# Block 1's second layer by seven half products, the turned keys of pairs 13 to 15 copied by ScalarE

## The chip, the core and the metric

The kernel runs on one core of one Trainium2 chip. The core's engines work side by side and wait for each other through semaphores: TensorE (PE in the profile, with its weight loads shown apart as PEld), VectorE (DVE), ScalarE (ACT), GpSimd (POOL) and SyncE (SP). Each engine takes its instructions strictly in the order in which the program lists them. SP and POOL also issue the DMA transfers; a DMA issue that has to wait holds up everything behind it in its engine's queue. The metric is the time in microseconds (us) of one execution of the whole program on the device, the median of several runs.

## What is computed

Eight batches (B) of eight heads (H) with 576 tokens (S) and 64 values a head. Attention over 16 "beacon" keys and the causal part of the 576 keys, then a mixer over the tokens of low rank (32), then a two-layer network of 512, 2048 and 512 channels:

```python
scores = scale * np.matmul(q, k_all.transpose(0, 1, 3, 2))   # k_all: 16 beacon keys, then 576
scores = np.where(causal, -1000000000.0, scores)
a = np.exp(scores - scores.max(-1, keepdims=True)); a /= a.sum(-1, keepdims=True) + 1e-09
x = np.matmul(a, v_all)                 # heads side by side: (8, 576, 512)
h = x.transpose(0, 2, 1) @ U @ V        # over the tokens, rank 32
u = x + h.transpose(0, 2, 1)
out = u + np.maximum(u @ w_ch1, 0.0) @ w_ch2
```

## The kernel before, in words

**Two kinds of work, interleaved by hand.** Attention goes by pairs of heads: four pairs (c = 0 to 3) in each of eight batches make pairs 0 to 31. The network goes by blocks of 512 tokens: nine blocks, 0 to 8, counted through all batches, so that block 1 needs batches 0 and 1. The work of a block is cut into units that stand in a list (`queue`); `fill(n)` takes the next n of them and emits their instructions. The attention's steps are written out by hand, and between them stand the fills: in `play` a letter f is one unit, q and k turn a pair's queries and keys, v is scores and exponentials, a and b are the two heads' products with the values, m is masks, r is a regrouping. A program order on every engine follows from that. `mix(b)` puts the mixer's units of batch b into the list and appends the blocks that become computable (`feed`).

**Turning queries and keys.** For pairs up to 15 a pair's queries and keys are first copied close together by VectorE (`regroup`, L290 and L292), then turned by TensorE into PSUM (L297), then copied from PSUM to `qT` and `kT` (`qkT_units`, L330; the 16 beacon columns by L335). `copies` in `qkT_of` says which engine copies: `copies[0]` is for the keys, `copies[1]` for the queries. Later batches are turned by DMA (`turns`, L869, on SP).

**A plain block** (`mlp_units`; blocks 0 and 1 before the change, by `FAST = 2` at L957). First layer: 16 units of four matmuls of 512 columns (L751), each with a Relu to f16 by ACT (L764) or DVE (L766). Second layer: 16 units of four matmuls of 512 columns (L777), 64 matmuls; four sums with the residual by DVE (L790; in block 0, copies by L792 and L794) and four stores by SP (L796), one for each 128 tokens.

**A fast block** (`fast_units`; blocks 2 to 8). The first layer is the same (L607, L618, L616). The second layer is a product of 2 x 2 quarters by seven half products instead of eight: A, F, B, C, D, E and D again, each of two units of eight matmuls of 256 columns (L633), 112 matmuls. They need sums of quarters of the hidden layer on DVE (L596, placed by the table `SUMS`), sums of quarters of the weights (`halves_of_w2`, L560, eight DVE instructions, once for the program, hung on units 16, 18, ... 30 of the last plain block) and sums of the products (`after`): one copy by ACT (L666), six sums by DVE (L654), then for each of four output tiles a sum with the residual by POOL (`residual`, L654 on POOL) and two stores by SP (`store`, L658). The units of the second layer are 14, of a plain block 16.

**What stands in SP's and POOL's queues around block 1.** POOL issues the loads of later batches: values (L239), beacons (L221), keys and queries (L852). These come one with each fill (`coming`). SP issues the stores, the DMA turning of the residual (`ut`, L583 or L745), the turning of keys and queries (L869), and the turning of attention's output `xb` into `uT` (L455, five instructions a batch), to which DVE adds the mixer's result (L476).

The lines that set this:

```python
            if t < FAST:
                units, state["part"] = mlp_units(512 * t, 512, dst, t % 2, t > 0)
                if t == FAST - 1:
                    for i, u in zip(range(NDC, 2 * NDC, 2), halves_of_w2()):
                        units[i] = lambda a=units[i], u=u: (a(), u())
            else:
                units = fast_units(512 * t, dst, t == NBLK - 1)
```

Of the kernel before, what the change touches and what calls it, by code (L numbers as in the profile page):

```python
# [30 lines left out]
def kernel(  # L31
# [21 lines left out]
    NH2 = H // 2  # L53
# [241 lines left out]
    def in_pair(pr):  # L295

        return [lambda ps, o, n, j, t=t: nc.tensor.transpose(ps[:, ds(o, n)], t[:n, j, :, :], ident[:n, :n]) for t in pr]  # L297

    def by_heads(st, c):

        def turn(ps, o, n, j, t):
            for h in range(2):
                nc.tensor.transpose(
                    ps[ds(D * h, D), ds(o, n)], t[:n, 2 * c + h, ds(D * j, D)], ident[:n, :n]
                )

        return [lambda ps, o, n, j, t=t: turn(ps, o, n, j, t) for t in st]
# [11 lines left out]
    def qkT_units(turns, qT, kT, c, copies=((nc.vector.tensor_copy,), (nc.vector.tensor_copy,)), apart=None):  # L319

        def one(i, dst, b0):
            w = TJ // len(copies[i])
            bs = 0 if apart else b0
            whole = dst[:, c, b0 : b0 + S].rearrange("x (p j) -> x p j", j=TJ)
            for a, copy in enumerate(copies[i]):
                ps = pst([P, TP * w + bs], F16, name="tps")
                for j in range(w * a, w * a + w):
                    n = TP + bs if j == TJ - 1 else TP
                    turns[i](ps, TP * (j - w * a), n, j)
                copy(  # L330
                    out=whole[:, :, ds(w * a, w)],
                    in_=ps[:, 0 : TP * w].rearrange("x (j p) -> x p j", j=w),
                )
                if bs and a == len(copies[i]) - 1:
                    copies[i][0](out=dst[:, c, 0:b0], in_=ps[:, TP * w : TP * w + b0])  # L335
                emptying(ps)
            if b0 and apart:
                beacons_apart(apart, dst, c, copies[i][0])

        return [lambda: one(1, qT, 0), lambda: one(0, kT, Nb)]  # L340
# [213 lines left out]
    def halves_of_w2():  # L554

        b11, b12 = w2[:, 0:HF, 0:HC], w2[:, 0:HF, HC:DM]
        b21, b22 = w2[:, HF:NDC, 0:HC], w2[:, HF:NDC, HC:DM]
        t1, t2, t3, t4 = (wt[:, i, :, :] for i in range(4))
        return [
            lambda o=o, x=x, y=y, h=h: nc.vector.tensor_tensor(  # L560
                out=o[:, ds(HF // 2 * h, HF // 2)], in0=x[:, ds(HF // 2 * h, HF // 2)],
                in1=y[:, ds(HF // 2 * h, HF // 2)], op=ALU.subtract,
            )
            for h in range(2) for o, x, y in ((t1, b12, b11), (t3, b22, b12), (t2, b22, t1), (t4, b21, t2))
        ]
# [332 lines left out]
    def regroup_of(p):  # L898
        b, c = divmod(p, NH2)
        prs[p] = [regroup(Ls[b][0], c, i, nc.vector.tensor_copy) for i in range(2)]  # L900
# [13 lines left out]
    def new_qT_of(p):  # L914
        b, c = divmod(p, NH2)
        if b not in qTs:
            new_qT(b)

    def qkT_of(p):
        b, c = divmod(p, NH2)  # L920
        new_qT_of(p)
        copies = [(act_copy, nc.vector.tensor_copy) if p == 0 else (nc.vector.tensor_copy,)] * 2
        turns = by_heads(Ls[b][0], c)
        for i, t in enumerate(prs.get(p, ())):
            if t is not None:
                turns[i] = in_pair(prs[p])[i]
        return qkT_units(turns, qTs[b], kTs[b % 2], c, copies, Ls[0][0][0] if p == 0 else None)
# [26 lines left out]
    DT0 = 4  # L954
    LAG = 10
    HINT = 5
    FAST = 2  # L957
    SUMS = {
# [14 lines left out]
    def fill(n):  # L973
        while n > 0 and queue:
            u = queue.pop(0)
            if u is not None:
                u()
            if coming:
                coming.pop(0)()
            n -= 1  # L980

    def feed(b):

        while state["t"] < NBLK and 512 * (state["t"] + 1) <= S * (b + 1):
            t = state["t"]
            dst = lambda i, m, t=t: rows[ds(512 * t + P * i, m), :]
# [27 lines left out]
    def play(line):  # L1014

        for word in line.split():
            what, p = word[0], int(word[1:].split(":")[0] or 0)
            if what == "f":
                fill(1)
            elif what in "qk":  # L1020
                qkT_of(p)["qk".index(what)]()
            elif what == "r":
                regroup_of(p)
            elif what in "ab":
                if what == "a":
                    avs[p] = av_of(p)
                avs[p]["ab".index(what)]()
            elif what in "mno":
                units = scores_of(p)
                units[2]() if what == "m" else units[3]("no".index(what))  # L1030
            elif what == "e":
                scores_of(p)[int(word[-1]) // 2]()
            elif what == "v":
                visit([(int(x[: x.index(":")]), int(g)) for x in word[1:].split(",") for g in x[x.index(":") + 1 :]])

    with tc.manual_schedule(engines={ENG.PE, ENG.Activation, ENG.DVE, ENG.SP, ENG.Pool}):
# [7 lines left out]
        prs[0][0] = regroup(first, 0, 0, V, act_copy, beacons=False)  # L1044
        idle(IDLE[0], plain)
        t0, sc = qkT_of(0), scores_of(0)
        t0[0]()
        idle(IDLE[4], ident)
# [3 lines left out]
        for u in qkT_of(1):  # L1052
            u()
# [83 lines left out]
        fill(8)  # L1137
        regroup_of(NP1)
        regroup_of(NP1 + 1)
        fill(8)  # L1140
        play("q8 f k8 f f v8:01 q9 f k9 f r10 v8:23,9:0 f")
        tr = []

# [206 lines left out]
```

## Time and profile before

| what | us |
|---|---|
| median of 3 runs | 343.74 |
| lowest and highest run | 340.02, 344.1 |
| the profiled execution, as timed | 340.93 |
| its span in the profile | 339.3 |
| busy in that span: PE, DVE, ACT, POOL | 329.8, 234.1, 178.7, 136.1 |

The profile is of one execution. A row of a timeline has start, duration and the instruction, with the idle time ahead of it in brackets and what ended it. A row of the chain of work has start, length and the instruction. A row of the groups by line has count, busy time and the mean of one in ns, then the idle time before. DMA issues stand under the queue that issues them (SPq, POOL); "DMA to landing" is from issue to the data's arrival. The clock of TensorE was granted in full (1.0) throughout. A matmul's duration in a row is longer than its distance to the next one, since matmuls are pipelined; the chain's rows give the distance.

### The profile page before, as it was taken

Reading aid. Unit: us, or ns where it says so; the run is one execution under the profiler, and the core shown is the slowest. Engines: PE = TensorE matmul, PEld = TensorE weight load, DVE = VectorE, ACT = ScalarE, POOL = GpSimd, SP = SyncE. Lnnn points to the kernel's source line nnn. Section 1 sums busy time; section 2 is a strip of 40 time slices with the busy share of each in tenths; the row PEclk is TensorE's granted clock in tenths of the full one; section 3 lists DMA queues with packets and bytes.
Section 4 is the critical chain, followed back from the end, with each engine's and each line's share of the span. In section 5 each row is a group of like instructions: output and inputs, shape, how many; then the busy total and the mean of one; then the engine's idle time right before and its main releaser. Section 6 shows DMA issues by size and latency. Waiting matters only on the chain.

```text
span 339.3 us, 8838 instructions
## 1 busy us (share of the span) xinstructions
PE 329.8 (97%) x3494; PEld 212.0 (62%) x3494; DVE 234.1 (69%) x585; ACT 178.7 (53%) x383; POOL 136.1 (40%) x175
## 2 busy tenths in 40 slices
PE   8799999999999999999999999999999999999993
PEld 4465655455555456865688888755875675585493
DVE  6586885689989748765876677687776963743652
ACT  5957951478851677257734784468445403502500
POOL 8986724765140900677066805040130014013041
PEclk9999999999999999999999999999999999999999
DMA  8999999999997994999999999944213304104113
GB/s 159 141 175 138 183 196 194 200 192 139 138 118 152 153 141 86 101 169 157 151 112 155 187 143 104 132 140 87 66 64 93 73 31 126 31 33 124 31 37 99
DMA packets 150832, 41.97 MB, mean 124 GB/s; under 512 B 132096, under 2 KB 149696, under 8 KB 150784
## 3 DMA queue, kind: packets, MB, share of 16 engines
q0 software_dynamic: 87568, 18.18, 74.6%
q1 hardware_dynamic: 62992, 22.87, 37.4%
q8 instruction: 29, 0.48, 0.6%
q10 hardware_dynamic: 224, 0.30, 0.3%
q14 instruction: 19, 0.16, 0.2%
HBM read 37.45 MB, written 9.44 MB: 138 GB/s over the span
## 4 chain that ended last, share of the span: by engine, by line
PE 88%; DMA 4%; POOL 3%; DVE 1%; issue 1%; ACT 1%; POOLq 0%; DVEq 0%
PE gps L607 29%; PE po L427 9%; PE mpsD L633 7%; PE cps L777 7%; PE gps L751 7%; PE sps L409 5%; DMA vs<-in_v_dram 4%; PE mpsF L633 4%; PE mpsC L633 4%; PE mpsA L633 4%; PE mpsB L633 4%; PE mpsE L633 3%; POOL vs L239 1%; PE sps L370 1%; POOL st L224 1%
## 5 line engine op out<-in xcount | busy, mean ns | idle before, releaser
L418 ACT ACTIVATE expt<-sps 128x496 f16<-128x496 f32 (+2 forms) x192 | 82.0, 539 | 52.6 <-PE sps L409 52.6
L607 PE MATMUL gps<-uT,w 128*128 128x512 f16 (+1 forms) x512 | 103.7, 353 | 0.0
L654 POOL TENSOR_TENSOR ob<-ob,ut 128x512 f32<-128x512 f32 x26 | 30.8, 1188 | 139.9 <-DVE ob L654 127.7
L633 PEld LDWEIGHTS <-gT 128*128 128x128 f16 x800 | 75.1, 98 | 11.3 <-issue 2.1
L618 ACT ACTIVATE gT<-gps 128x512 f16<-128x512 f32 x84 | 49.7, 609 | 58.8 <-PE gps L607 54.3
L607 PEld LDWEIGHTS <-w 128*128 128x128 f16 x512 | 47.6, 98 | 41.4 <-issue 1.6
L239 POOL DMA_DIRECT2D vs<-in_v_dram x50 | 39.7, 804 | 15.3 <-DMA w<-in_moe_w_ch_dram 12.3
L596 DVE TENSOR_TENSOR gT<-gT 128x1024 f16<-128x1024 f16 (+2 forms) x77 | 39.5, 540 | 4.2 <-ACT gT L618 3.3
L427 PEld LDWEIGHTS <-expt 128*128 128x128 f16 x900 | 33.9, 98 | 10.9 <-issue 2.7
L427 PE MATMUL po<-vs,expt 128*128 128x65 f16 x900 | 36.5, 194 | 1.1 <-DMA vs<-in_v_dram 1.0
L616 DVE TENSOR_SCALAR gT<-gps 128x512 f16<-128x512 f32 x28 | 19.3, 691 | 24.0 <-PE gps L607 23.4
L436 DVE TENSOR_TENSOR xb<-po,rec 128x320 f16<-128x320 f32 x64 | 31.4, 491 | 2.2
L751 PE MATMUL gps<-uT,w 128*128 128x512 f16 x128 | 32.5, 379 | 0.1
L777 PE MATMUL cps<-w,gT 128*128 128x512 f16 x128 | 31.1, 379 | 0.0
L435 DVE RECIPROCAL rec<-po 128x5 f32<-128x5 f32 x64 | 12.1, 189 | 19.0 <-PE po L427 18.7
L346 DVE TENSOR_TENSOR expt<-expt,bigmask 128x512 f16<-128x512 f16 x54 | 22.5, 417 | 1.2 <-ACT expt L418 1.2
L409 PE MATMUL sps<-qT,kT 64*128 64x80 f16 (+4 forms) x288 | 22.6, 281 | 0.0
L376 ACT ACTIVATE expt<-sps 128x496 f16<-128x496 f32 (+2 forms) x48 | 20.4, 564 | 0.6 <-PE sps L370 0.6
L409 PEld LDWEIGHTS <-kT 64*128 64x128 f16 x288 | 10.2, 94 | 13.4 <-issue 9.3
L777 PEld LDWEIGHTS <-gT 128*128 128x128 f16 x128 | 11.2, 98 | 11.6 <-issue 1.3
L852 POOL DMA_DIRECT2D st<-in_q_dram x20 | 16.9, 874 | 3.2 <-DVE expt L348 1.4
L751 PEld LDWEIGHTS <-w 128*128 128x128 f16 x128 | 10.6, 97 | 10.8 <-issue 1.2
(125 smaller groups left out, 384.8 us busy)
## 6 DMA issues: line engine op xcount, KB each, us to landing
out_dram<-ob SPq DMA_DIRECT2D x55, 128.0 KB, 1.9
vs<-in_v_dram POOLq DMA_DIRECT2D x18, 128.0 KB, 7.9
w<-in_moe_w_ch_dram POOLq DMA_DIRECT2D x4, 512.0 KB, 6.4
w<-in_moe_w_ch_dram POOLq DMA_DIRECT2D x2, 1024.0 KB, 12.8
out_dram<-ob SPq DMA_DIRECT2D x8, 256.0 KB, 4.9
st<-in_k_dram POOLq DMA_DIRECT2D x12, 128.0 KB, 7.2
st<-in_q_dram POOLq DMA_DIRECT2D x12, 128.0 KB, 8.3
st<-in_k_dram POOLq DMA_DIRECT2D x4, 288.0 KB, 11.9
```

The costliest lines, as they stand in the source:

```text
L239: nc.gpsimd.dma_start(out=dst[a : a + nq[j], j, :, :], in_=src[hs, ds(q0[j], nq[j]), :].rearrange("h p d -> p h d"))
L409: nc.tensor.matmul(banks[i][:, ds(at0 + o, w)], kT[hp, c, ds(P * ch, P)], qT[hp, c, ds(qa, w)], start=True, stop=True, skip_group_check=le ...
L418: nc.scalar.activation(out=at[p][3][i][:, ds(SLOT * g, gw[g])], in_=bank[:, ds(at0, gw[g])], func=AF.Exp, scale=scale)
L427: nc.tensor.matmul(po[:, j, :], ex[0 : nk[c], ds(blk[(c, j)], P)], vs[0 : nk[c], ds(c * H * E + h * E, E)], start=(c == 0), stop=(c == j),)
L436: nc.vector.tensor_tensor(out=xb[:, :, ds(h * D, D)], in0=po[:, :, 0:D], in1=r.broadcast_to([P, NT, D]), op=ALU.mult)
L596: nc.vector.tensor_tensor(out=o[:, ds(d0, n)], in0=x[:, ds(d0, n)], in1=y[:, ds(d0, n)], op=op)
L607: nc.tensor.matmul(g[:, ds(o, w)], w1[:, cc, ts(dc, P)], uT[:, cc, ds(at, w)], start=(cc == 0 and o == 0), stop=(cc == NCC - 1), skip_grou ...
L618: nc.scalar.activation(out=cell["g"][:, dc, :], in_=g, func=AF.Relu)
L633: nc.tensor.matmul(ps, a()[:, d, ds(P * i, P)], bm[:, d, ds(c0, w)], start=fresh and d == 0 and (i == 0 or key != bank), stop=d == HF - 1, ...
L654: eng.tensor_tensor(out=out, in0=x, in1=y, op=ALU.add)
L751: nc.tensor.matmul(g[:, 0:n], w1[:, cc, ts(dc, P)], uT[:, cc, ds(r0, n)], start=(cc == 0), stop=(cc == NCC - 1))
L777: nc.tensor.matmul(ps[:m, :], gT["t"][:, dc, ds(P * i, m)], w2[:, dc, :], start=(dc == 0), stop=turned and dc == NDC - 1, skip_group_check ...
```

## The change

Three edits. `FAST` becomes 1, so that block 1 is a fast block: its second layer is done by the seven half products, and the eight sums of the weights' quarters move to the units of block 0's second layer. The keys of pairs 13, 14 and 15 (`p > (DT0 - 1) * NH2` is p > 12) are copied from PSUM by ACT instead of DVE. The fill after the regroupings of pairs 8 and 9 is 6 units long instead of 8, since a fast block has two units fewer.

```diff
@@ -920,6 +920,8 @@
         b, c = divmod(p, NH2)
         new_qT_of(p)
         copies = [(act_copy, nc.vector.tensor_copy) if p == 0 else (nc.vector.tensor_copy,)] * 2
+        if p > (DT0 - 1) * NH2:
+            copies[0] = (act_copy,)
         turns = by_heads(Ls[b][0], c)
@@ -954,7 +956,7 @@
-    FAST = 2
+    FAST = 1
@@ -1137,7 +1139,7 @@
         fill(8)
         regroup_of(NP1)
         regroup_of(NP1 + 1)
-        fill(8)
+        fill(6)
         play("q8 f k8 f f v8:01 q9 f k9 f r10 v8:23,9:0 f")
```

In the changed program, with block 1 fast, SP's queue has eight half stores (L658) where four whole ones (L796) stood, and POOL's queue has four more sums. POOL's queue then reads: the beacons of the keys of batch 5, the sum of the first output tile, the five key loads and the first query load, the second tile's sum, two query loads, the third tile's sum, the last two query loads, the fourth tile's sum. SP's queue reads: the eight stores, one `ut` turning, then the turning of keys (one) and queries (four), three more of `ut`, and then the five of `xb` (L455) for the next blocks. TensorE has 48 matmuls and 48 weight loads more than before.

## The prediction

> **What bounds the kernel now.** I read the page's shares first, then the waits of TensorE, then the chain of work and the windows around block 1.
>
> ```profile
> span 339.3 us, 8838 instructions
> PE 329.8 (97%) x3494; PEld 212.0 (62%) x3494; DVE 234.1 (69%) x585; ACT 178.7 (53%) x383; POOL 136.1 (40%) x175
> PE 88%; DMA 4%; POOL 3%; DVE 1%; issue 1%; ACT 1%; POOLq 0%; DVEq 0%
> ```
>
> TensorE is busy 97% of the span and holds 88% of the chain that ended last. A saved matmul is saved time only as long as nothing that TensorE waits for comes late. The windows show how much room there is: columns are PE, weight loads, DVE, ACT and POOL busy, then clock, DMA share and GB/s.
>
> ```profile
> 50.25:69.50 19.25, 19.25 (x164) 10.31 (x160) 11.89 (x26) 6.18 (x14) 10.62 (x14) 1.00 1.72 203
> 69.50:94.70 25.20, 24.68 (x315) 13.69 (x312) 22.04 (x64) 20.16 (x46) 12.35 (x16) 1.00 2.09 146
> 94.70:113.40 18.70, 18.70 (x168) 9.43 (x165) 17.75 (x42) 7.44 (x19) 5.83 (x8) 1.00 1.39 135
> 113.40:148.10 34.70, 34.70 (x374) 22.85 (x373) 23.91 (x57) 20.79 (x46) 13.08 (x16) 1.00 1.40 116
> PE tps L297 <- DVE gT L766: 0.5, 1, 0.5
> ```
>
> They are the second layer of block 0, the first and the second layer of block 1, and all of block 2. TensorE has no gap in three of them, and 0.5 us behind DVE in the other. So the stretch of the change gains what TensorE saves, and what comes late there or behind it costs in full.
>
> **The change, part by part.**
>
> *The matmuls.* From the chain of work (start, length):
>
> ```profile
> 107.55 2.59 PE cps L777 x12
> 132.77 1.75 PE mpsA L633 x16
> ```
>
> A matmul of 512 columns takes 2.59 / 12 = 0.216, one of 256 columns 1.75 / 16 = 0.109. Block 1 gives up 64 x 0.216 = 13.8 and gets 112 x 0.109 = 12.25: **-1.57 us**. The first layer keeps its matmuls.
>
> [...]
>
> *The weights' sums on DVE, moved into block 0's second layer.*
>
> ```profile
> L560 DVE TENSOR_TENSOR wt<-w 128x1024 f16<-128x1024 f16 x4 | 2.7, 680 | 0.0
> L596 DVE TENSOR_TENSOR gT<-gT 128x1024 f16<-128x1024 f16 x35 | 23.5, 683 | 3.4 <-ACT gT L618 3.3
> L596 DVE TENSOR_TENSOR gT<-gT 128x768 f16<-128x768 f16 x21 | 11.4, 553 | 0.6
> L596 DVE TENSOR_TENSOR gT<-gT 128x256 f16<-128x256 f16 x21 | 5.5, 287 | 0.2
> L790 DVE TENSOR_TENSOR ob<-cps,ut 128x512 f32<-128x512 f32 x4 | 2.7, 686 | 0.6 <-PE cps L777 0.6
> L330 DVE COPY kT<-tps 128x576 f16<-128x576 f16 x15 | 11.3, 751 | 1.6 <-PE tps L297 0.7 <-PE tps L303 0.7
> ```
>
> Eight at 0.68 = 5.4 us join 11.89 in the window of 19.25: 17.3, still under. What hides them is DVE's idle time there. If an insertion delays a turned key by its length, TensorE waits 0.7; all eight badly placed would be 5.4. I take 0, because the one wait of this kind in the trace is 0.5, and keep 0 to 5.4 for the range. Below zero is excluded, since TensorE has no gap in that window.
>
> *The hidden layer's sums on DVE in block 1.* 35 / 7 = 5, 3 and 3 of the three sizes: 3.4 + 1.7 + 0.9 = 6.0, and six sums of products at 0.69 = 4.1. Away go four L790 (2.7), two Relus (12 L766 in two blocks is six each, a fast block has four: 1.4), the eight weight sums (5.4) and three key copies at 0.75, with their beacon columns (0.16 each: 2.7). Net -2.1 on DVE in the stretch 69.5 to 113.4, where it was busy 39.8 of 43.9. Cost 0: DVE's idle 4.1 hides it. If a sum of the hidden layer is late at its product, TensorE waits for that one piece, 0.29 to 0.68.
>
> *The shorter fill.* Pairs 8 to 15 take their steps up to two units earlier (1.7). The loads that they read do not come earlier, and one regrouping was just in time:
>
> ```profile
> 66.42 9.05 DMA vs<-in_v_dram
> 75.49 0.68 DVE pr L292
> ```
>
> A wait of up to 1.7 on DVE could come of it. TensorE's next reader stood 0.5 behind it already, so the bounds are 0 and 1.7; I take 0, since the chain names a transfer of values there and not the keys' own.
>
> *The key copies on ACT.* The trace has no such copy of 576 columns. The nearest are ACT's Relu of 512 columns at 0.609 and the 96 x 384 copy at 0.523, so 0.5 to 0.75 each, and a second instruction of at most 0.37 (its exponential of 208 columns): at most 3.4 for three. ACT was busy 27.6 of 43.9. Such a copy may stand behind a run of exponentials of 2.9 (six of them at 92.86 in the timeline):
>
> ```profile
> L618 ACT ACTIVATE gT<-gps 128x512 f16<-128x512 f32 x84 | 49.7, 609 | 58.8 <-PE gps L607 54.3 <-issue 4.3
> L893 ACT ACTIVATE pr<-stkq 96x384 f16<-96x384 f32 x2 | 1.0, 523 | 1.0 <-DMA stkq<-in_q_dram 0.7 <-DMA stkq<-in_k_dram 0.3
> L418 ACT ACTIVATE expt<-sps 128x208 f16<-128x208 f32 x48 | 13.2, 368 | 37.1 <-PE sps L409 37.1
> 92.86 2.91 ACT L418 ACTIVATE expt<-sps 128x496 f16<-128x496 f32 x6
> ```
>
> Its reader is the pair's scores, several units of 0.86 later. I take 0; the bounds are 0 and one run of exponentials, 2.9.
>
> *The four sums on POOL and the eight stores on SP.* Here I expect the bill. POOL's sums stand between the loads of batch 5; SP's stores wait for them, and behind the stores stand the turning of keys and queries and then of `xb` (L455), which DVE's L476 needs. First POOL, SP, then DVE and PE of the trace before:
>
> ```profile
> 114.31 4.22 POOL L852 DMA_DIRECT2D st<-in_q_dram  x5
> 138.02 1.15 POOL L654 TENSOR_TENSOR ob<-ob,ut 128x512 f32<-128x512 f32 x1 [13.54 <-DVE ob L654]
> 139.12 4.23 POOL L239 DMA_DIRECT2D vs<-in_v_dram  x5
> 109.62 0.54 POOL L221 DMA_DIRECT2D st<-in_beacon_k_dram  x1 [12.87 <-DMA kT<-st]
> 114.29 0.33 SPq L796 DMA_DIRECT2D out_dram<-ob  x1
> 146.49 5.30 SPq L658 DMA_DIRECT2D out_dram<-ob  x8
> 114.71 1.24 SPq L583 DMA_TRANSPOSE ut<-uT  x1
> 117.35 1.19 SPq L869 DMA_TRANSPOSE kT<-st  x1
> 120.80 5.94 SPq L869 DMA_TRANSPOSE qT<-st  x4
> L455 SPq DMA_TRANSPOSE uT<-xb x5: 1250/1264/1803, 131.2 to 137.0; - x5
> 139.94 2.41 DVE L476 TENSOR_TENSOR uT<-ups,uT 128x496 f16<-128x496 f32 x4
> 142.89 0.68 DVE L654 TENSOR_TENSOR kept<-mpsC,kept 128x512 f32<-128x512 f32 x1
> 144.69 0.69 PE sps L409 x8
> ```
>
> POOL: the beacon load is released by turned keys, which stand behind attention's output on SP; that comes up to two first-layer units earlier (1.7 us), so at 107.9 instead of 109.6. From there 0.54, a sum of 1.15, five key loads and one query load at 0.84 (5.1), a sum, two loads (1.7), a sum, two loads, a sum: 13.5, to 121.4. SP: the last two stores wait for that and take between 0.33 (a store at 114.29) and 0.66 (5.30 for eight), 1.0 for both, to 122.4; `ut` 1.24, keys 1.25: the first query turning issues at 124.9 instead of 120.80, **4.1 late**. L455 follows in the same queue; its fourth, at 137.0 - 1.3 = 135.7, moves to 139.8. L476 waits for the fourth (the fifth is for the short end). TensorE meanwhile is 1.57 early: DVE wants L476 at 139.94 - 1.57 = 138.4.
>
> How long does such a turning take to land? Three stretches show it: beside value loads (issued from 92.6), in quiet, and the key turnings beside value loads (from 139.12).
>
> ```profile
> 92.56 4.19 POOL L239 DMA_DIRECT2D vs<-in_v_dram  x5 [0.38 <-issue]
> DMA to landing us min/median/max: 4.5/5.6/8.2
> DMA to landing us min/median/max: 2.3/2.5/2.9
> DMA to landing us min/median/max: 2.3/7.2/8.3
> ```
>
> The changed program issues value loads at 139.12 - 1.57 = 137.5, so the fourth L455 now falls 2.3 behind their start. Before, it was 3.4 ahead. Quiet ends: 142.3, DVE waits 3.9. Beside loads, 5.6 to 8.3: 145.4 to 148.1, a wait of 7.0 to 9.7. What is queued behind L476 on DVE: the sum of product C, whose bank the scores at 144.69 take. It ended at 142.89 + 0.68 = 143.57, so 1.1 of lateness is covered and the rest stops TensorE: 2.8 in quiet, 5.9 to 8.6 beside loads. I take 6.8 (a landing of 6.5, between the two contended medians 5.6 and 7.2), because the row nearest in time is contended.
>
> [...]
>
> **Sum.** -1.57 + 6.8 = +5.2 against this execution: 340.93 + 5.2 = 346.1. The median shown is 2.8 above this execution, and with three runs I can't say how much of that is chance; I put a third of it on top: **347.0**.
>
> **Rivals.**
> - *The turnings land as in quiet.* For it: value loads may be slow to start. Then -1.57 + 2.8 = +1.2: 342.1. [...] The trace speaks against (7.2).
> - *Faster: the lateness stays within its cover, and the saving stands.* Place: L476; it decides if the fourth L455 lands before 138.4 + 1.1 = 139.5, that is if SP is late by under 1.3 instead of 4.1. For it: block 2 before has the same eight stores behind POOL's sums, and TensorE does not wait in the next stage. Against it: in that stage SP's list has L455 ahead of the keys and queries, here behind. Time 340.93 - 1.57 = 339.4, up to 342.2 on the median.
> - *Worse: another wait on top*, the weights' sums delaying the turned keys of pairs 8 and 9 (up to 5.4), keys on ACT behind exponentials (2.9), or a regrouping that waits for its load (1.7). For it: 17.3 of 19.25 on DVE. Against: DVE idles between these very copies. About 3 to 5 more: 349.5 to 352.
>
> **How the numbers follow.** Chances: forecast 0.5, quiet 0.2, faster 0.17, worse 0.13. The range reaches from inside the faster case to the contended upper bound on the median, 343.74 - 1.57 + 8.6 = 350.8: 341 to 351; it leaves out the lower half of the faster case and most of the worse one. The forecast's own range is 345 to 351. About 2% (6.9 us) can be told from no change: over 2% slower needs the upper end of the forecast or the worse case, 0.17; over 2% faster nothing gives, 0.01; within 0.82.
>
> **What would show it.** Right: 112 matmuls at L633 in block 1 at 0.109; the query turning of SP near 125; a DVE idle of some 7 us ahead of L476 near 138, ended by the DMA of `uT`; TensorE idle by 5 to 8 us between 140 and 150, put down to DVE at L476. The stretch up to block 2 shorter by 1.6. Wrong: L476 without idle ahead, value loads or L455 issued at other times, TensorE's gaps in block 0's second layer or at pairs 13 to 15.

## The result, and the profile after

The changed kernel takes **351.16 us** (median of five runs, 350.98 to 353.0), the kernel before 343.74 (five runs, 340.02 to 348.03). The ratio is **1.0271, 95% interval 1.0203 to 1.0339**: slower by 2.7%, where 347.0 and a range of 341 to 351 were forecast. The kernel before spreads widely, so all ratios here leave the longest executions of a kernel out, while medians keep them.

The profiled execution took 351.16, with a span of 349.5. First the page of the changed kernel: its span, and the rows of TensorE's busy share and granted clock in 40 slices (a slice is 8.7 us).

```profile
span 349.5 us, 8964 instructions
PE   8899999999999999279999999999999999999992
PEclk9999999999999999969999999999999999999997
```

Two slices stand out. The one that starts near 140 has TensorE at 2 tenths, and the next has the clock at 6 tenths. Next, what TensorE and then DVE waited for in the changed kernel (us in total, times, longest).

```profile
PE mpsE L633 <- DVE uT L476: 8.1, 1, 8.1
PE tps L297 <- DVE pr L290: 0.9, 2, 0.7
```

```profile
DVE uT L476 <- DMA uT<-xb: 11.2, 1, 11.2
```

That is the forecast's chain: TensorE waits for L476 on DVE, and that waits for the turned `xb`. Now the queues behind it, POOL and SP in the timeline of the changed kernel (start, duration, and in brackets the idle time ahead), with the landing times of L455.

```profile
109.68 0.54 POOL L221 DMA_DIRECT2D st<-in_beacon_k_dram  x1 [14.53 <-DMA kT<-st]
122.09 1.25 POOL L654 TENSOR_TENSOR ob<-ob,ut 128x512 f32<-128x512 f32 x1
137.70 4.21 POOL L239 DMA_DIRECT2D vs<-in_v_dram  x5
```

```profile
111.47 12.71 SPq L658 DMA_DIRECT2D out_dram<-ob  x8
126.97 5.97 SPq L869 DMA_TRANSPOSE qT<-st  x4
136.96 7.93 SPq L455 DMA_TRANSPOSE uT<-xb  x5
DMA to landing us min/median/max: 6.1/7.2/8.0
```

POOL's last sum ends at 123.34. SP's eight stores hold the queue for 12.71 us, up to 124.18, since the last of them waits for that sum. The query turnings then issue at 126.97 (120.80 before), and L455 starts at 136.96 (131.19 before), beside the value loads of 137.70. It lands in 7.2 instead of 2.5.

Where the 10.2 us between the two spans (349.5 and 339.3) lie is read from five rows of TensorE's timeline: the first products of the first layer in blocks 0, 2 and 3, product E of block 2 and the last product D. Before, then after:

```profile
23.12 1.02 PE L751 MATMUL gps<-uT,w 128*128 128x512 f16 x4
113.36 1.03 PE L607 MATMUL gps<-uT,w 128*128 128x512 f16 x4
143.66 1.04 PE L633 MATMUL mpsE<-wt,gT 128*128 128x256 f16 x8
147.95 1.03 PE L607 MATMUL gps<-uT,w 128*128 128x512 f16 x4
332.16 1.93 PE L633 MATMUL mpsD<-w,gT 128*128 128x256 f16 x24
```

```profile
22.59 1.02 PE L751 MATMUL gps<-uT,w 128*128 128x512 f16 x4
111.90 1.03 PE L607 MATMUL gps<-uT,w 128*128 128x512 f16 x4
150.49 1.87 PE L633 MATMUL mpsE<-wt,gT 128*128 128x256 f16 x8 [8.13 <-DVE uT L476]
156.92 1.03 PE L607 MATMUL gps<-uT,w 128*128 128x512 f16 x4
341.14 1.93 PE L633 MATMUL mpsD<-w,gT 128*128 128x256 f16 x24
```

| stretch | before | after | difference |
|---|---|---|---|
| start to block 0's first layer | 23.12 | 22.59 | -0.53 |
| from there to block 2 | 90.24 | 89.31 | -0.93 |
| block 2 to block 3 | 34.59 | 45.02 | **+10.43** |
| block 3 to the last product | 184.21 | 184.22 | +0.01 |
| from there to the end of the span | 7.14 | 8.36 | +1.22 |

The whole bill lies in one stage, and two small sums beside it were not in the forecast: a gain of 0.93 instead of 1.57, and an end that is 1.22 longer.

### The profile page after: what moved, and what is told of

The parts are those of the page before. It is cut to its first block, busy times and chain, and to the rows that moved or that the text cites. A ratio compares the mean times of both kernels' runs of the same rounds, so it can differ in the third digit from the quotient of the medians.

```text
span 349.5 us, 8964 instructions
## 1 busy us (share of the span) xinstructions
PE 330.5 (95%) x3542; PEld 216.8 (62%) x3542; DVE 238.1 (68%) x590; ACT 182.0 (52%) x392; POOL 140.6 (40%) x179
## 4 chain that ended last, share of the span: by engine, by line
PE 87%; DMA 4%; DVE 3%; POOL 2%; issue 1%; SPq 1%; ACT 1%; DVEq 0%; POOLq 0%
PE gps L607 32%; PE po L427 8%; PE mpsD L633 8%; PE sps L409 6%; PE mpsF L633 4%; PE mpsB L633 4%; PE mpsA L633 4%; PE mpsE L633 4%; PE gps L751 4%; PE cps L777 4%; PE mpsC L633 4%; DMA uT<-xb 2%; DMA vs<-in_v_dram 1%; PE tps L297 1%; PE sps L370 1%
## 5 line engine op out<-in xcount | busy, mean ns | idle before, releaser
L607 PE MATMUL gps<-uT,w 128*128 128x512 f16 (+1 forms) x576 | 120.0, 355 | 0.2 <-DVE xb L436 0.2
L654 POOL TENSOR_TENSOR ob<-ob,ut 128x512 f32<-128x512 f32 x30 | 35.3, 1180 | 151.2 <-DVE ob L654 125.4
L618 ACT ACTIVATE gT<-gps 128x512 f16<-128x512 f32 x96 | 57.1, 611 | 63.8 <-PE gps L607 57.6
L607 PEld LDWEIGHTS <-w 128*128 128x128 f16 x576 | 52.8, 98 | 46.5 <-issue 2.0
L596 DVE TENSOR_TENSOR gT<-gT 128x1024 f16<-128x1024 f16 (+2 forms) x88 | 45.5, 542 | 4.2 <-ACT gT L618 3.3
L616 DVE TENSOR_SCALAR gT<-gps 128x512 f16<-128x512 f32 x32 | 22.1, 691 | 24.4 <-PE gps L607 23.8
L633 PE MATMUL mpsE<-wt,gT 128*128 128x256 f16 x128 | 17.0, 282 | 8.1 <-DVE uT L476 8.1
L476 DVE TENSOR_TENSOR uT<-ups,uT 128x496 f16<-128x496 f32 x24 | 14.5, 666 | 11.7 <-DMA uT<-xb 11.2
L852 POOL DMA_DIRECT2D st<-in_k_dram x20 | 16.9, 856 | 0.7 <-DMA st<-in_q_dram 0.7
L751 PE MATMUL gps<-uT,w 128*128 128x512 f16 x64 | 16.2, 379 | 0.1
```

The lines of the kernel that those rows point to most:

```text
L596: nc.vector.tensor_tensor(out=o[:, ds(d0, n)], in0=x[:, ds(d0, n)], in1=y[:, ds(d0, n)], op=op)
L607: nc.tensor.matmul(g[:, ds(o, w)], w1[:, cc, ts(dc, P)], uT[:, cc, ds(at, w)], start=(cc == 0 and o == 0), stop=(cc == NCC - 1), skip_grou ...
L618: nc.scalar.activation(out=cell["g"][:, dc, :], in_=g, func=AF.Relu)
L633: nc.tensor.matmul(ps, a()[:, d, ds(P * i, P)], bm[:, d, ds(c0, w)], start=fresh and d == 0 and (i == 0 or key != bank), stop=d == HF - 1, ...
L654: eng.tensor_tensor(out=out, in0=x, in1=y, op=ALU.add)
L751: nc.tensor.matmul(g[:, 0:n], w1[:, cc, ts(dc, P)], uT[:, cc, ds(r0, n)], start=(cc == 0), stop=(cc == NCC - 1))
```

## The experiments

The theory: POOL's sums hold SP's stores, these hold the turnings (first keys and queries, then `xb`), and `xb` now lands beside the value loads; L476 comes late, and TensorE stands still. Rivals: the copies on ACT cost it; the sums of the weights do; the loss is work and not waiting; or only one of lateness and contention matters.

### Each link of the chain by itself

*b_noact* takes the copies on ACT out of the changed kernel:

```
-        if p > (DT0 - 1) * NH2:
-            copies[0] = (act_copy,)
```

> The changed kernel with the key copies of pairs 13 to 15 back on DVE. Queue theory (POOL's sums hold SP's stores, these hold the turning of xb at L455, TensorE stands still for L476): the copies play no part, so the wait for mpsE at L633 stays at 8.1 us within 1 and the time stays within 0.5% of the changed kernel's 351.2. Rival (copies on ACT cost it): the wait shrinks and up to 3 us come back, 348.

Measured: 352.17, ratio 1.0316 (1.0256 to 1.0375); the wait for L476 is 7.2. The copies play no part in the loss that can be measured.

*c_turns* changes only the order of SP's queue: the five turnings of batch 5's first keys and queries go behind those of `xb`.

```
-            if c in (0, NH2 - 1) and b + 1 == DT0:
+            if c == 0 and b + 1 == DT0:
                 fill_turns(tr, NT)
```

> The changed kernel with the five turnings of batch 5's first keys and queries (L869) put behind the turnings of xb (L455) in SP's queue, not ahead of them. Queue theory: L455 issues from about 126 to 130 instead of 136.96, ends ahead of the value loads of 137.70, and lands some 2.5 us after issue; L476 no longer waits, TensorE's 8.1 us of idle and the about 2.3 us at half clock behind it go: 351.2 - 10.4 = 340.8, a ratio to before of 0.99 to 1.00. A price can come up where the turned queries are then wanted, since they turn later. Rival (the turnings of xb are late for another reason, or the loss is work and not waiting): the ratio stays at 1.02 or above.

Measured: 341.53, ratio **0.9996** (0.9968 to 1.0023). SP and TensorE in its timeline:

```profile
123.05 6.10 SPq L583 DMA_TRANSPOSE ut<-uT  x4
129.27 6.86 SPq L455 DMA_TRANSPOSE uT<-xb  x5
136.31 1.92 SPq L869 DMA_TRANSPOSE kT<-st  x1
```

```profile
142.04 1.04 PE L633 MATMUL mpsE<-wt,gT 128*128 128x256 f16 x8
146.33 1.03 PE L607 MATMUL gps<-uT,w 128*128 128x512 f16 x4
```

L455 has been issued before the value loads begin (137.54) and lands in 2.5 (median), and product E runs without idle ahead of it. From 111.75, its first product of block 2, the stage takes 34.58, as before. One place in a queue is worth ten microseconds, and no price of the later queries shows: from block 3 to the last product it is 184.36 (184.21 before).

*d_vlate* leaves SP late but issues batch 5's value loads one slot later, so that L455 lands alone.

```
-            if c == (1 if b >= DT0 else 0) and b + 1 < B:
+            if c == (2 if b == DT0 else 1 if b >= DT0 else 0) and b + 1 < B:
                 load_batch(b + 1)
```

> The changed kernel with batch 5's value loads issued one slot later, so that the turnings of xb no longer land beside them; SP's lateness stays. If lateness and contention share the bill: the landing of L455 falls from 7.2 to about 2.5, L476 starts some 4.8 us earlier, TensorE's idle falls from 8.1 to about 3.3, and if the half clock behind it comes of a long idle, its 2.3 go as well: 344 to 346. If lateness alone does it: the idle stays at 8 and the time at 351. If contention alone does it: no idle, 341. The later values can cost something of their own where block 3 begins.

Measured: 347.98, ratio 1.0206 (1.0131 to 1.0281). The landing falls to 2.5, DVE's wait from 11.2 to 5.4, TensorE's idle to 2.33: lateness and contention share the bill, as expected. But the clock was expected to stay up with the shorter idle, and it did not, so the time misses the 344 to 346. First the landing times of L455, then rows of TensorE's timeline, then its windows (length, busy time, matmuls, granted clock, DMA share, GB/s):

```profile
DMA to landing us min/median/max: 2.4/2.5/3.2
```

```profile
144.68 1.54 PE L633 MATMUL mpsE<-wt,gT 128*128 128x256 f16 x8 [2.33 <-DVE uT L476]
152.77 1.03 PE L607 MATMUL gps<-uT,w 128*128 128x512 f16 x4
```

```profile
142.00:144.00 2.00, 0.35 (x4) 1.00 0.53 106
144.00:146.00 2.00, 1.32 (x8) 0.76 0.25 45
146.00:148.00 2.00, 2.00 (x8) 0.50 0.65 128
150.00:152.00 2.00, 2.00 (x11) 0.53 0.59 167
152.00:154.00 2.00, 2.00 (x26) 1.00 0.68 210
```

TensorE is busy again from 144.68, and the clock still halves: at 146 - 2 x (1 - 0.76) / 0.5 = 145.04, until 150 + 2 x 0.47 / 0.5 = 151.88, which is 6.84 us. So here the half clock falls on work, and takes back 1.96 (table below) of what the shorter idle saved.

*e_dve* makes block 1's four residual sums on DVE, so that the stores do not wait for POOL.

```
-            add(obs[name], obs[name], u_of(h, c), nc.gpsimd)
+            add(obs[name], obs[name], u_of(h, c), nc.vector if t0 == 512 else nc.gpsimd)
```

> The changed kernel with block 1's four residual sums on DVE instead of POOL (4 of about 0.7, 2.8 us of DVE work more). Queue theory: SP's last stores no longer stand behind POOL's loads, SP's L455 comes back to about 132 to 135, ahead of the value loads, and the wait of 8.1 at mpsE goes nearly or wholly, the half clock with it: 341 to 344. Rival (SP is held by the stores' number or the turnings' order, not by POOL's sums): L455 still issues at 137, and the time stays at 350 or above.

Measured: 342.86 (runs of 340.88 to 350.79), ratio 1.0026 (0.9982 to 1.007); no wait for L476 in the profiled execution. Its SP:

```profile
119.32 6.43 SPq L869 DMA_TRANSPOSE qT<-st  x4
130.84 6.42 SPq L455 DMA_TRANSPOSE uT<-xb  x5
```

With the same eight stores in the same place, L455 is at 130.84 (before: 131.19). It is POOL's sums between its loads that hold SP, not the number of stores.

### How much the clock costs

*h_fill* (on the changed kernel, 64) and *i_fill* (on d_vlate, 18) put matmuls of zeros into TensorE's idle; they add zero to product D's bank.

```
+            if k == 4 and j == 1 and t0 == 1024:
+                for _ in range(64):
+                    nc.tensor.matmul(
+                        banks["D"][0 : NC * P - SK, 0, :], kTs[0][:, 0, SK : NC * P], w2[:, 0, 0:HC],
+                        start=False, stop=True, skip_group_check=True,
+                    )
```

> The changed kernel with 64 matmuls of zeros (48 columns wide, 256 rows moved, added to product D's bank) behind product D's first half of block 2, where TensorE stands idle for 8.1 us. At 0.109 each they fill 7.0 of it. Nothing waits less: L476 is as late as before. Clock theory (TensorE's idle halves its own clock for 6.8 us, worth about 2.3 here): the granted clock stays 1.00 from 140 to 160, and 2 us come back: 349. Rival (the clock falls for another reason, or zeros do not count): the clock is 0.50 from 147 to 154 as before, and the time stays at 351 or above. If the matmuls lengthen the path themselves, 353 or more.

Measured: 348.48, ratio 1.0204 (1.0123 to 1.0286), and the clock row has no dip. The number is as expected, but the trace says that little of it is the clock; that the number fits is luck. The clock row of its page, then TensorE and DVE in its timeline:

```profile
PEclk9999999999999999999999999999999999999998
```

```profile
111.49 1.03 PE L607 MATMUL gps<-uT,w 128*128 128x512 f16 x4
141.87 7.17 PE L721 MATMUL mpsD<-w,kT 128*48 128x256 f16 x64
148.09 2.42 DVE L476 TENSOR_TENSOR uT<-ups,uT 128x496 f16<-128x496 f32 x4 [9.95 <-DMA uT<-xb]
148.97 1.05 PE L633 MATMUL mpsE<-wt,gT 128*128 128x256 f16 x8
150.56 0.37 PE L409 MATMUL sps<-qT,kT 64*128 64x496 f16 x1 [0.24 <-DVE uT L476]
151.78 0.75 PE L409 MATMUL sps<-qT,kT 64*128 64x464 f16 x2 [0.21 <-DVE kept L654]
155.10 1.03 PE L607 MATMUL gps<-uT,w 128*128 128x512 f16 x4
```

From product E to block 3's first product, the kernel before takes 147.95 - 143.66 = 4.29. h_fill takes 155.10 - 148.97 = 6.13 **at full clock**, the changed kernel 156.92 - 150.49 = 6.43 at half. So 1.84 of the 2.1 lost there is DVE's backlog: the scores trickle behind L476 and the sum of product C, one bank at a time. In the changed kernel the half clock costs 0.3 at most. Of the 3.0 between the two spans (349.5 and 346.5), 1.41 lie in this stage, where L476 was late by 9.95 and not 11.20; 1.18 are a shorter end, and 0.41 lie ahead of block 2.

> The kernel with batch 5's value loads one slot later (347.98; TensorE idle 2.3 us for L476, then 0.50 of the clock for 6.83 us from 145.05), with 18 matmuls of zeros put into that idle (18 x 0.109 = 2.0). Clock theory: the half clock is what the rest of its loss is made of, 6.83 x 0.5 = 3.4 us: with the idle filled the clock stays 1.00 and the time falls by 3.4 to about 344.5. Rival (an idle this short does not halve the clock, something else does): clock and time stay as they are, 348.

Measured: 346.75, ratio 1.0127 (1.0034 to 1.022), runs of 345.16 to 349.33. The profiled execution (347.91) has 0.7 of idle left, and its clock halves nonetheless, later, from 148.2 to 155.0. The runs at a mean clock of 0.997 and 0.993 took 345.16 and 345.58, near the 344.5 expected; those at 0.990 and 0.989 took 347.91 and 349.33. So the size of the clock's part fits. What brings the half clock on is not shown: here the longest idle ahead of it was 0.72, while h_fill kept its clock with gaps of 0.2 to 0.3, and the rival (something else than the idle halves it) is not refuted.

### Single parts on the kernel before

*f_halves* only moves the weights' sums into block 0 (`if t == FAST - 1` becomes `if t == 0` with FAST still 2); *a_act* only has the two lines of b_noact added.

> The kernel before with one part of the change: the eight sums of quarters of the second layer's weights (L560) are made between block 0's second-layer units and not block 1's; block 1's second layer stays whole products. Theory (the price forecast as 0 was a wait of some 0.7 at a regrouping of turned keys in block 0): a ratio of 1.000 to 1.003, and a wait of TensorE for DVE's pr of 0.5 to 1 us between 60 and 70. Rival (it costs up to its work, 5.4): a ratio of up to 1.016.

> The kernel before with one part of the change: the key copies of pairs 13 to 15 on ACT. Forecast and theory: no effect, a ratio within 0.997 to 1.003. Rival (copies behind exponentials, up to 2.9 us): a ratio of up to 1.008, with a wait of TensorE's scores for ACT's kT.

Measured: f_halves 345.71, ratio 1.002 (0.9973 to 1.0066); a_act 342.94, ratio 0.9981 (0.9926 to 1.0036). Neither part moves the time by what can be measured, and the wait for `pr` between 60 and 70 that was expected in f_halves is not there. Their profiled executions (348.16 and 347.57) are longer than their medians and show something else. f_halves, DVE and TensorE:

```profile
144.75 2.42 DVE L476 TENSOR_TENSOR uT<-ups,uT 128x496 f16<-128x496 f32 x4 [5.65 <-DMA uT<-xb]
```

```profile
112.44 1.03 PE L607 MATMUL gps<-uT,w 128*128 128x512 f16 x4
145.47 1.03 PE L633 MATMUL mpsE<-wt,gT 128*128 128x256 f16 x8 [2.58 <-DVE uT L476]
154.40 1.30 PE L607 MATMUL gps<-uT,w 128*128 128x512 f16 x4
```

This program has no stores behind POOL's sums, and yet the same wait. Its POOL got to L221 at 111.05, and SP's query turnings issued at 124.10 instead of 120.80: 3.3 us were enough to push L455 (134.41) into the value loads of 138.19. a_act shows the same: L221 at 111.90, queries at 124.37, an idle of 3.00. So the order of SP's queue is a weak point without the seven products too. That the long runs of the kernel before come from it is not shown, since none of them was profiled; j_turns0 below speaks for it.

All these traces obey one sum. L476's wait on DVE less the cover of 1.1 that the forecast found, and the clock's part (from E to block 3, less h_fill's 6.13), against what the stage from block 2 to block 3 takes beyond 34.59:

| kernel | wait - 1.1 | clock | sum | stage beyond 34.59 |
|---|---|---|---|---|
| after | 10.1 | 0.3 | 10.4 | 10.43 |
| b_noact | 9.2 | 0.2 | 9.4 | 9.55 |
| h_fill | 8.85 | 0 | 8.85 | 9.02 |
| d_vlate | 4.3 | 1.96 | 6.3 | 6.29 |
| f_halves | 4.55 | 2.8 | 7.35 | 7.37 |
| a_act | 4.97 | 2.13 | 7.1 | 7.12 |
| i_fill | 4.77 | 2.8 | 7.57 | 7.59 |
| c_turns | none beyond cover | 0 | 0 | -0.01 |
| e_dve | none beyond cover | 0 | 0 | -0.01 |

The clock column is a remainder. So the sum tests one thing: within 0.2, in every trace with a wait, product E comes later than in the kernel before (counted from block 2) by the wait of L476 less 2.94, and 1.84 of backlog follow it.

### Is a better version in it?

*j_turns0* is the kernel before with c_turns' reordering; *c2_turns* is c_turns once more beside it; *k_early* is c_turns with the sums of the weights behind units 16 to 22 and 24 (`zip((16, 17, 18, 19, 20, 21, 22, 24), halves_of_w2())`).

> The kernel before with nothing but the same reordering: the five turnings of L869 behind those of L455. Block 1's second layer is whole products again. Two longer profiled executions (f_halves, a_act) show TensorE waiting 2.6 and 3.0 us for L476 in the old layout too, where the query turnings came at 124.1 and 124.4 instead of 120.80. If the queue's order is the weak point by itself: this kernel is freed of the longer executions, its median lies at 340 to 342 and its fast ones are within 0.3% of before's. If the reordering has a price (queries turned later): a ratio of 1.005 or more. Beside the changed kernel with the same reordering it gives the seven products' own worth: 1.57 us less up to block 2 by the forecast's matmul term, if no wait eats it.

> The changed kernel with the turnings of L869 behind those of L455 once more, now beside the kernel before with the same reordering on the same chip. If the seven products are worth their 1.57 us (less at most 0.7 for the weights' sums): 0.9 to 1.6 us below that kernel, a ratio to before of 0.994 to 0.998. If the sums eat it all: equal, 0.999 to 1.002.

> The reordered changed kernel with the sums of the weights (L560) put earlier in block 0's second layer, behind units 16 to 22 and 24 and no longer behind every second unit up to 30, so that none stands between the regroupings of keys near 65. If these sums cost the 0.7 us of waiting for pr at a regrouping: 0.7 below c2_turns, a ratio to before of 0.992 to 0.996, the best of all. Rival: they now hold up the casts of the first mixing (L478, near 52 to 55), whose readers are TensorE's next products: equal or up to 1 us above c2_turns.

Measured on one chip, where the kernel before had a median of 346.17 (29 runs): j_turns0 **340.93**, ratio 0.9973 (0.9933 to 1.0013); c2_turns 341.03, ratio 0.9996 (0.9958 to 1.0034); k_early 341.39, ratio 0.9988 (0.9945 to 1.003). The reordering brings either kernel to 341, and the long runs of the kernel before (19 of the 29 above 343, up to 350.66) are rare with it: eleven of j_turns0's twelve lie at 342.63 or below. By the ratios none is faster than before beyond their intervals. The seven products are worth nothing that can be measured here, and the earlier sums in k_early do not bring the 0.7 that was hoped for (its median is 0.4 above c2_turns'). From block 0's first product c2_turns reaches block 2 in 89.05 us and j_turns0 in 89.92, but in these two profiles the end takes it back. SP's last stores and DVE's last sum, in j_turns0 (span 338.3), then in c2_turns (span 338.9):

```profile
331.12 4.48 SPq L658 DMA_DIRECT2D out_dram<-ob  x7
333.08 0.29 DVE L654 TENSOR_TENSOR ob<-mpsD,kept 128x128 f32<-128x128 f32 x1 [0.16 <-PE mpsD L633]
```

```profile
330.50 5.33 SPq L658 DMA_DIRECT2D out_dram<-ob  x7
332.46 0.29 DVE L654 TENSOR_TENSOR ob<-mpsD,kept 128x128 f32<-128x128 f32 x1 [0.15 <-PE mpsD L633]
```

From the last sum to the end it is 338.3 - 333.37 = 4.9 and 338.9 - 332.75 = 6.15. Two kernels look for the cause in the length of SP's stream: *l1_merge* makes block 1's eight stores four, *l2_merge* halves them in every block but the last.

```
+            if i is None and t0 == 512:
+                nc.sync.dma_start(
+                    out=dst(2 * h, 2 * P)[:, ds(HC * c, HC)].rearrange("(k p) c -> p k c", p=P), in_=obs[name]
+                )
+                return
             for k in range(2) if i is None else (i,):
```

> c2_turns with block 1's eight stores made as four, each of both row groups of a tile, so that SP's stream is as long as that of the kernel before. If the number of SP's instructions ahead of the end is what lengthens the last stores (one of the seven taking 0.86 to 1.24 us instead of 0.38): the end from the last DVE sum falls from 6.1 to about 4.9, and the time by 0.9: 340.1. Rival (the end is longer for another reason): SP's last seven stores still take 5.2 and the time stays at 341.

> c2_turns with two stores made one in every block but the last (24 to 28 fewer on SP). Each removed store frees SP of 0.33 to 0.66 us, none of which TensorE waits for any more: no gain beyond that of l1_merge, 340 to 341; if SP's length sets the last stores' time, it falls at some other place of the stream and the end can be 4.9 or 6.1. A price can come of larger transfers that end later, but nobody reads them.

Measured: l1_merge 342.31, ratio 0.9989 (0.9952 to 1.0026); l2_merge 340.98, ratio 0.9971 (0.9933 to 1.001). From the last sum to the end: 6.9 and 6.4. The number of SP's instructions is not the cause. What is stays open: all kernels with seven products in block 1 have an end of 5.85 to 6.88, except the two with matmuls of zeros 190 us earlier (4.92 and 4.83); no run here says why.

## Why the forecast was right and wrong

Direction and mechanism were right, the place, the engine and the instruction too; the size was not (+5.2 forecast against the profiled execution, +10.2 measured). By its steps:

- *Matmuls* (-1.57): block 2 is reached 0.93 sooner. On this stretch TensorE's listed waits are 0.92 (0.68 at 66.46 for a regrouping, `tps` L297 behind `pr`, above; 0.24 at 84.09) against 0.52 before: 0.4 of the 0.64 that are missing. The rest lies in gaps too short to be listed.
- *The shorter fill* and *the weights' sums on DVE*, both taken as 0: the 0.68 at 66.46 goes with the shorter fill (bounds of 0 and 1.7) rather than with the sums. f_halves moves the sums and keeps the fill of 8, and has no listed wait in block 0's second layer. k_early keeps the fill of 6 and has all its sums ahead of 62, and still waits 0.3 there. Ten of the eleven kernels with the fill of 6 have this wait, of 0.3 to 0.7. No run has the shorter fill alone, so its own price stays open.
- *The hidden layer's sums*, *the key copies on ACT*: no cost shows, for the copies (0.68 each on ACT) in b_noact and a_act.
- *The four sums on POOL and the eight stores on SP*: this is the step that failed, in its sizes. L476's wait was put at 7.9 and was 11.20. In the chain of waits the deciding L455 issues at 141.89 and takes 7.32:

```profile
141.89 7.32 DMA uT<-xb
149.76 0.69 DVE uT L476
```

It issues 2.1 later than forecast (139.8), of which 1.8 are that POOL's L221 did not come earlier (109.68, not 107.9; 107.5 to 110.0 in the experiments with seven products). The forecast had L221 follow attention's output; but on SP four query turnings of batch 4 stand ahead of that output's turnings, and they issued at 87.16, as in the kernel before (87.15). In the runs with seven products where they issued by 86.3, L221 came at 107.5 to 108.6. The landing took 0.8 more than 6.5. From the landing (149.21) to L476 (149.76) go 0.55 that the sum left out, and DVE was ready at 138.56, not 138.4: 2.1 + 0.8 + 0.55 - 0.16 = 3.3. The cover of 1.1 was right. TensorE stopped one product earlier than forecast, at product E, which takes a bank that the first L476 frees.
- Not in the sum at all: the half clock (0.3) and the longer end (1.22), against a start of this execution that was 0.53 earlier.

So: 5.2 + 3.3 + 0.3 + 0.64 (the smaller gain) + 1.22 - 0.53 = 10.1 of the 10.2. Of the rivals, quiet landings are refuted (7.2 beside loads; 2.5 in d_vlate), and the faster case failed at its own condition, an SP late by under 1.3: it was late by 6.2. The worse case (349.5 to 352) has the measured time in it, but only by luck: the keys on ACT cost nothing that shows, and the waits for regroupings came to 0.9 and not to 3 to 5. The third of 2.8 that was put on top for the median was not needed, for 351.16 is both the median and the profiled execution. The upper bound of 351 took contended landings in, but not a later POOL and the end with them.

## What to carry to other kernels

Before lengthening one queue's wait, list everything behind it in order and ask which entry has the nearest reader: moving the five entries with a far reader behind the five with a near one was worth ten microseconds, more than the arithmetic saved. In these traces a stall that is late by X costs X less the cover of the next reader (1.1 here), whatever engine shows the idle, and a half clock behind it adds to that only where work, not waiting, falls into it (0.3 at most in the changed kernel, 1.96 in d_vlate). A program whose runs spread by 3% may have such an edge already: a profile of one of the longer runs can show it.

## What the hardware showed that was not expected

The clock's half state lasted the same in each of the executions in which it was read: 147.36 to 154.19 in the changed kernel (6.83 us), 145.04 to 151.88 in d_vlate (6.84), 145.85 to 152.68 in b_noact, and 6.82 to 6.83 in i_fill, f_halves and a_act too. The changed kernel's windows at its ends:

```profile
147.00:147.50 0.50, 0.00 (x0) 0.86 1.93 200
147.50:148.00 0.50, 0.00 (x0) 0.50 1.78 112
153.50:154.00 0.50, 0.50 (x2) 0.50 0.03 8
154.00:154.50 0.50, 0.50 (x3) 0.81 0.00 0
```

No run shows what sets this length. In d_vlate the clock halved, at 145.04, behind an idle of 2.33 us (8.13 in the changed kernel), and it stayed halved until 151.88 although TensorE was busy from 144.68 on.

The same turnings landed in 2.5 us alone and in 7.2 beside value loads (5.7 in b_noact, 6.4 in h_fill), and with the loads moved they were back at 2.5 (d_vlate).
